# mLSTM cell and mixture of depths: exponents one step later, operands at the ends of steps, tables in the prologue, the tail in pieces

## The chip, the cores and the metric

One NeuronCore of a Trainium2 chip runs the kernel as one program. Its engines run side by side: TensorE (PE; its weight loads are listed as PEld), VectorE (DVE), ScalarE (ACT), GpSimd (POOL), and SyncE (SP), which issues most of the DMAs. Each engine takes its own instructions strictly in the order in which they were written; between engines, semaphores order them. The metric is the device time of one execution in microseconds (us).

## The reference, cut to what matters

Two blocks follow each other: a recurrent mLSTM cell over B=4, H=8, S=768, D=40, and a mixture-of-depths layer on its output x, seen as (4, 768, 320).

```python
# per batch and head, for t in 0..767
m_new  = max(f[t] + m, i[t]);  f_stab = exp(f[t] + m - m_new);  i_stab = exp(i[t] - m_new);  m = m_new
C = f_stab * C + i_stab * outer(v[t], k[t]);   n = f_stab * n + i_stab * k[t]
y[t] = sigmoid(o[t]) * (C @ q[t]) / max(abs(n @ q[t]), 1)
# then per batch, on x = y as (768, 320)
scores = x @ w_gate;   top = the 128 positions with the largest scores
out[top] = x[top] + sigmoid(scores[top]) * (relu(x[top] @ w1) @ w2);   out elsewhere = x
```

## The kernel before

The recurrence is computed by chunks of 128 positions, so there are 24 **steps** `(b, c)`: 4 batches of 6 chunks, numbered n = 0 to 23. All 8 heads of a chunk are handled together. A step is written by `step(n)`, and it works on three chunks at once: it ends chunk n, prepares the products of chunk n+1, and turns and weighs chunk n+2. No scheduler moves anything: the order in which the code is written is the order on each engine.

In a step, TensorE does in this order: `within` (L383, tile `pH`, 32 matmuls, the chunk's own attention), `exchange` for n+1 (L352 and L358, tile `pIC`: the carried state `C` against the queries, and the new part of the state from the scaled values `wv`), `products` (L326, `pS`, queries by keys), `weights` for n+2 (L304, `pW`, the exponents of the decay weights, from two operands `a_o` and `M_o`), in some steps `operands` (L234, `pO`, six small matmuls that place gate rows into those operands), then a piece of the mixture layer (`layer`: `pcol`, `pidx`, `pX`, `ph`, `py`, or `warm`, three matmuls into `pw` that nobody reads), the transposes of chunk n+2 (L284, `pt`) and `spread` (L412, `pb`, this chunk's scores as a row).

ScalarE takes the exponential of `pW` into `W` (L305), turns `pO` into `a_o` (L238) and `M_o` (L245, four instructions), copies `pt` into `T` (L285), applies the output gate to `so` (L295, L296), and copies `pb` into `sb` (L413). GpSimd zeroes the upper triangle of `W` (`causal`, L310), scales the values (`stated`, L317, `wv`), decays the state (`decay`, L340, `C`) and multiplies the gate by the reciprocal denominator (L398, `sor`). VectorE does the rest: `norm` (L390 to L396), `compare` (L419, `ge`, which scores are beaten), `result` (L403 `x`, L406 `sc`), `weighted` (L332, `P` = `pS` times `W`, which `pH` of the next step needs), and `exchanged` (L365 `num`, L375 `C`).

The operands of one chunk number c serve a pair of batches: `operands(0, c)` batches 0 and 1, `operands(1, c)` batches 2 and 3. The first kind is made in the prologue and in steps 1 to 3, the second in steps 4 to 9. They need tables `place`, of which the second pair is made on GpSimd after step 2 (L685 to L688). In steps 1 to 3 (`late`), the exponents of chunk n+2 are written at the end of the step, and `causal` and `stated` of that chunk behind them; in all other steps they stand in the middle.

PSUM holds 8 banks. `ps_t` has two buffers that `pt` and `pW` share, `ps_m` two that `pO`, `pb`, `pcol`, `pidx`, `pX`, `ph` and `py` share. A matmul into a shared buffer waits until its last reader is done.

After step 23 comes the tail (L712 to L740): the last comparison over all six chunks, ranks from counts and column sums (`pcol`), one-hot selections `sel`, the selected rows transposed by matmul (`pX`, L729), and the two layers of the last batch (`ph` L491, `py` L500).

Of the kernel before, what the change touches and what calls it, by code (L numbers as in the profile page):

```python
# [27 lines left out]
def kernel(  # L28
# [380 lines left out]
    def spread(u, sc, sb):  # L409

        pb = ps_m.tile([128, L], FP, name="pb", tag="m")
        nc.tensor.transpose(pb, sc[:, u:u + 1].to_broadcast([128, L]), ident)  # L412
        nc.scalar.copy(out=sb[:, u, :], in_=pb)  # L413

    def compare(u, sc, sb, ge, cnt):
# [5 lines left out]
                                       op0=OP.is_ge, op1=OP.mult, accum_out=cnt[:, u:u + 1])  # L421

    def columns_of(ge):

# [1 line left out]
        for t in reversed(range(NT)):
            for u in reversed(range(t, NT)):
                nc.tensor.matmul(pcol[:, t:t + 1], ge[:, GE[u] + t * L:GE[u] + (t + 1) * L], ones_b, start=(u == NT - 1),
                                 stop=(u == t))
# [253 lines left out]
    for n in range(2, N):  # L683
        step(n)
        if n == 2:  # L685
            for j in range(2):
                nc.gpsimd.memset(place[j][1], 0.0)
            places(1)  # L688
# [78 lines left out]
```

## Time and profile before

| | before |
|---|---|
| runs | 209.55, 209.54, 208.18 us, median 209.54 us |
| profiled execution, its own time | 209.95 us |
| its span, first to last instruction | 207.8 us |
| outside the span | 2.15 us |
| mean granted TensorE clock | 0.983 of full speed |
| PE busy | 180.4 us, 87% of the span |
| PEld busy | 148.2 us, 71% |
| DVE busy | 143.3 us, 69% |
| ACT busy | 102.8 us, 49% |
| POOL busy | 98.8 us, 48% |

A step can be read off the trace by the start of its `pH`. Steps 10 to 22 are nearly full on TensorE; the waits in front of TensorE stand in steps 1 to 9 and in the tail. In a row, the bracket at the end is the idle time of that engine just before the row, and what ended it.

### The profile page before, as it was taken

How to read it: one execution, taken by the hardware profiler on the slowest of the kernel's cores; microseconds unless marked ns; L12 is line 12 of the kernel's file. 1: busy time of each engine (PE TensorE's matmuls, PEld its weight loads, DVE VectorE, ACT ScalarE, POOL GpSimd, SP SyncE). 2: the span in 40 equal slices, each digit the busy share in tenths (PEclk: the TensorE clock that was granted, in tenths of full speed). 3: DMA queues.
4: the chain of work that ended last, by engine and by line, in shares of the span. 5: the costliest groups of instructions: out<-in, count | busy, mean ns of one | idle time of the engine just before them, and what ended most of it. 6: DMA issues, size and time to landing. Idle time of an engine off the chain costs nothing.

```text
span 207.8 us, 6508 instructions
## 1 busy us (share of the span) xinstructions
PE 180.4 (87%) x2597; PEld 148.2 (71%) x2606; DVE 143.3 (69%) x408; ACT 102.8 (49%) x246; POOL 98.8 (48%) x152
## 2 busy tenths in 40 slices
PE   6988877877698777979999999899999998988990
PEld 2467755656486756868887888788887897958870
DVE  7759964647885867765688869976886898664101
ACT  5682553935936864756555365546545543200210
POOL 6087406093646537533485466365657572022201
PEclk9999969999969999999999999999999999999999
DMA  4999999928999999994999689578992101010100
GB/s 82 122 172 141 143 182 169 153 29 196 155 180 166 214 145 238 160 155 51 159 139 148 104 148 166 106 126 119 145 152 65 36 32 35 32 35 33 32 0 32
DMA packets 105854, 24.37 MB, mean 117 GB/s; under 512 B 100640, under 2 KB 105248, under 8 KB 105824
## 3 DMA queue, kind: packets, MB, share of 16 engines
q1 hardware_dynamic: 105296, 22.60, 70.9%
q0 software_dynamic: 384, 1.31, 2.2%
q8 instruction: 20, 0.33, 0.8%
q14 instruction: 10, 0.08, 0.2%
q10 hardware_dynamic: 144, 0.05, 0.1%
HBM read 19.37 MB, written 4.59 MB: 115 GB/s over the span
## 4 chain that ended last, share of the span: by engine, by line
PE 33%; DVE 18%; issue 10%; POOL 7%; ACT 3%; DMA 3%; POOLq 1%; ACTq 0%
PE pH L383 8%; PE ph L491 5%; PE pS L326 5%; POOL sor L398 4%; PE pt L284 4%; PE py L500 3%; DVE P L332 3%; PE pIC L352 3%; ACT W L305 3%; DVE scr L406 2%; DVE num L390 2%; DVE x L403 2%; DVE den L394 2%; DVE ge L419 2%; DMA out_dram<-ye,idx 1%
## 5 line engine op out<-in xcount | busy, mean ns | idle before, releaser
L310 POOL TENSOR_SCALAR_AFFINE_SELECT W<-W 128x512 f32<-128x512 f32 x48 | 32.1, 693 | 34.0 <-ACT W L305 33.7
L305 ACT ACTIVATE W<-pW 128x512 f32<-128x512 f32 x48 | 26.1, 596 | 41.9 <-POOL sor L398 15.7
L398 POOL TENSOR_TENSOR sor<-so,rec 128x320 f32<-128x320 f32 x24 | 22.4, 934 | 41.4 <-DVE rec L396 40.0
L285 ACT COPY T<-pt 128x512 f32<-128x512 f32 x48 | 26.1, 595 | 18.1 <-PE pt L284 18.0
L332 DVE TENSOR_TENSOR P<-pS,W 128x512 f32<-128x512 f32 x48 | 30.7, 679 | 0.8 <-POOL W L310 0.8
L383 PEld LDWEIGHTS pH<-v,P 128*64 128x64 f32 x768 | 24.8, 138 | 7.3 <-DVE P L332 2.7
L383 PE MATMUL pH<-v,P 128*64 128x64 f32 x768 | 28.3, 226 | 1.7 <-DVE P L332 1.7
L326 PE MATMUL pS<-T 64*128 64x128 f32 x384 | 28.8, 291 | 0.0
L284 PE MATMUL pt<-ident,qk 128*128 128x128 f32 x192 | 26.0, 279 | 0.7 <-ACT W L305 0.7
L284 PEld LDWEIGHTS pt<-ident,qk 128*128 128x128 f32 x192 | 22.7, 144 | 5.1 <-ACT W L305 1.6
L326 PEld LDWEIGHTS pS<-T 64*128 64x128 f32 x384 | 24.1, 193 | 1.4
L491 PE MATMUL ph<-xeT,w 128*128 128x128 f32 x192 | 23.8, 280 | 1.5 <-ACT a_o L238 1.2
L491 PEld LDWEIGHTS ph<-xeT,w 128*128 128x128 f32 x192 | 22.1, 192 | 3.2 <-issue 1.4
L390 DVE TENSOR_TENSOR num<-num,pH 128x328 f32<-128x328 f32 x20 | 9.9, 495 | 17.6 <-PE pH L383 17.4
L403 DVE TENSOR_TENSOR x<-num,sor 128x320 f32<-128x320 f32 x20 | 11.1, 553 | 13.4 <-POOL sor L398 13.4
L419 DVE SCALAR_TENSOR_TENSOR ge<-sb,sc,earlier 128x128 bf16<-128x128 f32 (+5 forms) x24 | 18.4, 768 | 1.9 <-ACT sb L413 1.9
L500 PE MATMUL py<-w,hT 128*128 128x320 f32 x64 | 19.1, 439 | 0.0
L352 PE MATMUL pIC<-C,T 128*64 128x82 f32 x320 | 15.2, 236 | 1.9 <-DVE C L375 1.1
L358 PE MATMUL pIC<-wv,qk 128*64 128x41 f32 x320 | 12.8, 229 | 3.4 <-POOL wv L317 3.4
L317 POOL TENSOR_TENSOR wv<-v,cols 128x328 f32<-128x328 f32 x20 | 15.0, 751 | 0.0
L352 PEld LDWEIGHTS pIC<-C,T 128*64 128x64 f32 x320 | 12.7, 137 | 2.6 <-issue 1.5
L176 PE MATMUL pw<-earlier 128*128 128x512 bf16 x30 | 12.5, 478 | 2.2 <-POOL earlier L98 1.6
(121 smaller groups left out, 265.4 us busy)
## 6 DMA issues: line engine op xcount, KB each, us to landing
qk<-in_k_dram SPq DMA_DIRECT2D x24, 160.0 KB, 3.5
qk<-in_q_dram SPq DMA_DIRECT2D x24, 160.0 KB, 4.4
v<-in_v_dram SPq DMA_DIRECT2D x24, 160.0 KB, 4.9
so<-in_o_gate_dram SPq DMA_DIRECT2D x24, 160.0 KB, 4.6
out_dram<-x SPq DMA_DIRECT2D x24, 160.0 KB, 1.9
w<-in_moe_w_dram SPq DMA_DIRECT2D x2, 640.0 KB, 4.7
w<-in_moe_w_dram SPq DMA_DIRECT2D x2, 512.0 KB, 3.8
w<-in_moe_w_dram SPq DMA_DIRECT2D x1, 256.0 KB, 4.0
```

What stands on the lines that cost most here:

```text
L284: nc.tensor.transpose(pt[:, p, :], qk[:, j, 2 * p:2 * p + 2, :].rearrange("s a d -> s (a d)"), ident)
L285: nc.scalar.copy(out=T[:, j], in_=pt)
L305: nc.scalar.activation(out=W[:, h0:h0 + 4, :], in_=pW, func=AF.Exp)
L310: nc.gpsimd.affine_select(out=W[:, h0:h0 + 4, :], in_=W[:, h0:h0 + 4, :], compare_op=OP.is_ge, fill=0.0, base=0, pattern=[[0, 4], [1, L]], ...
L326: nc.tensor.matmul(pS[j][:, p, :], T[e, 0, p, :], T[e, 1, p, :], start=True, stop=True)
L332: nc.vector.tensor_tensor(out=P[:, :, j, :], in0=pS[j], op=OP.mult, in1=W.rearrange("p (n a) t -> p n a t", a=2)[:, :, j, :])
L352: nc.tensor.matmul(pI[t, 2 * p * D1:2 * (p + 1) * D1], T[:, 1, p, t], C[:, p].rearrange("e a d -> e (a d)"), start=True, stop=True)
L383: nc.tensor.matmul(pH[t, 2 * p + j, :], P[:, p, j, t], v1[:, 2 * p + j, :], start=True, stop=True)
L398: nc.gpsimd.tensor_tensor(out=sor, in0=so, in1=rec.unsqueeze(2).to_broadcast([128, H, D]), op=OP.mult)
L419: nc.vector.scalar_tensor_tensor(out=ge[:, GE[u]:GE[u + 1]], in0=sb.rearrange("p t l -> p (t l)")[:, 0:n], scalar=sc[:, u:u + 1], in1=earl ...
L491: nc.tensor.matmul(self.ph[:, f % 4, :], w1[:, j, f * 128:(f + 1) * 128], self.xeT[:, j, :], start=(j == 0), stop=(j == NDC - 1))
L500: nc.tensor.matmul(self.py, self.hT[:, f, :], w2[:, f, :], start=(f == 0), stop=(f == NFC - 1))
```

## The change

The change moves work and splits some of it; it leaves the arithmetic of the result as it was.

- **Exponents one step later.** `weights` of chunks 3, 4 and 5 stood at the end of steps 1, 2 and 3. Now they stand in steps 2, 3 and 4, right behind that step's `pH`, and their `causal` behind that step's `norm`. `stated` of these chunks (`wv`) no longer stands behind their `causal`.
- **Operands at the ends of six steps.** `operands(1, c)` moves from the middle of steps 4 to 9 to the end of steps 3 to 8, behind `spread`.
- **Tables in the prologue.** The second pair of `place` tables is zeroed on VectorE and filled on GpSimd in the prologue; two of three zeroings of `C` go.
- **Prologue.** Chunk 1's transposes come ahead of its exponents.
- **Tail in pieces.** The last `spread` and its copy go. The last comparison is split in two, the second read from PSUM; column sums over chunks 0 to 4 come early, those of chunk 5 go into a tile of their own (`pend`); the selection is made in six pieces instead of three; `pX` becomes three tiles, each copied as soon as it is there. Step 23 takes six of the eight `py` pieces instead of five.

```diff
@@ prologue
-    for j in range(2):
-        nc.vector.memset(place[j][0], 0.0)
+    for u in range(B // 2):
+        for j in range(2):
+            nc.vector.memset(place[j][u], 0.0)
...
     places(0)
-    for C in C_t:
-        nc.gpsimd.memset(C, 0.0)
+    nc.gpsimd.memset(C_t[1], 0.0)
+    places(1)
@@ step(n)
+        late = 0 < n < NT - 2
+        if 1 < n < NT - 1:
+            W[n + 1] = weights(*steps[n + 1])
         if n + 1 < N:
             give = exchange(*steps[n + 1], loaded[n + 1][0], T[n + 1], wv[n + 1])
...
-        if 4 <= n < 4 + NT:
-            operands(1, n - 4, beside=False)
         num, sor = norm(nums.get(n), pH, so)
+        if 1 < n < NT - 1:
+            causal(W[n + 1])
...
             if not late:
-                weighed(n + 2)
-        spread(c, *state[b][1][:2])
-        if late:
-            W[n + 2] = weights(*steps[n + 2])
+                causal(W[n + 2])
+            if n != 1:
+                stated(n + 2)
+        if n + 1 < N:
+            spread(c, *state[b][1][:2])
+        if 3 <= n < 3 + NT:
+            operands(1, n - 3, beside=False)
...
-        if late:
-            weighed(n + 2)
+        if n == 1:
+            stated(n + 2)
@@ tail
-    compare(u, sc, sb, ge, cnt)
-    own.second(5, NFC)
-    rank = ranks(columns_of(ge), cnt)
+    nc.vector.tensor_tensor(out=base[:, 0:u], in0=cnt[:, 0:u], in1=later[:, 0:u], op=OP.add)
+    sums_of(pcol, ge, u)
+    nc.vector.scalar_tensor_tensor(out=ge[:, GE[u]:GE[u] + n], ... accum_out=before)
+    nc.tensor.transpose(pb, sc[:, u:u + 1].to_broadcast([128, L]), ident)
+    own.second(6, NFC)
+    nc.vector.scalar_tensor_tensor(out=ge[:, GE[u] + n:GE[u + 1]], in0=pb, ... accum_out=cnt[:, u:u + 1])
+    for t in range(NT):
+        nc.tensor.matmul(pend[:, t:t + 1], ge[:, GE[u] + t * L:GE[u] + (t + 1) * L], ones_b, start=True, stop=True)
+    nc.vector.tensor_tensor(out=base[:, 0:u], in0=base[:, 0:u], in1=pcol, op=OP.subtract)
+    nc.vector.scalar_tensor_tensor(out=base[:, u:u + 1], in0=cnt[:, u:u + 1], scalar=before, in1=later[:, u:u + 1], ...)
+    nc.vector.tensor_tensor(out=rank, in0=base, in1=pend, op=OP.subtract)
...
-    for t in range(0, NT, 2):
-        select(sel, rank, t, t + 2)
+    for t in range(NT):
+        select(sel, rank, t, t + 1)
...
+        if j < 2:
+            copies[j](out=last.xeT[0:w, j], in_=pX[j][0:w])
     own.leave()
     select(sel_h, rank, 0, NT)
-    nc.scalar.copy(out=last.xeT[:, 0:NDC - 1], in_=pX[:, 0:NDC - 1])
-    nc.scalar.copy(out=last.xeT[0:w, NDC - 1], in_=pX[0:w, NDC - 1])
+    copies[2](out=last.xeT[0:w, 2], in_=pX[2][0:w])
```

On TensorE, around the end of step 2 and the start of step 3, there stood in the order before (`v_115` is chunk 3's value tile, `a_o_701` and `M_o_700` the operands of chunk 4):

```order
L284 MATMUL pt<-ident,qk_111 128x128 x8
L412 MATMUL pb<-ident,sc 128x128
L304 LDWEIGHTS a_o_701
L304 MATMUL pW<-M_o_700,a_o_701 128x512
L304 LDWEIGHTS a_o_701
L304 MATMUL pW<-M_o_700,a_o_701 128x512
L383 MATMUL pH<-v_115,P 64x64 x16
L352 MATMUL pIC<-C_118,T 64x82 x8
L358 MATMUL pIC<-wv,qk_111 64x41 x8
```

and there stands now:

```order
L286 MATMUL pt<-ident,qk_111 128x128 x8
L414 MATMUL pb<-ident,sc 128x128
L385 MATMUL pH<-v_115,P 64x64 x16
L306 LDWEIGHTS a_o_705
L306 MATMUL pW<-M_o_704,a_o_705 128x512
L306 LDWEIGHTS a_o_705
L306 MATMUL pW<-M_o_704,a_o_705 128x512
L354 MATMUL pIC<-C_118,T 64x82 x8
L360 MATMUL pIC<-wv,qk_111 64x41 x8
```

`pH` has moved ahead of the two `pW`; the same holds one step earlier, from step 1 into step 2.

On GpSimd, from `sor` of step 1 to `sor` of step 3, there stood before (`v_115` and `v_116` are chunks 3 and 4):

```order
L398 TENSOR_TENSOR sor<-so,rec 128x320
L310 AFFINE_SELECT W<-W 128x512 x2
L317 TENSOR_TENSOR wv<-v_115,cols_636 128x328
L340 TENSOR_TENSOR C_118<-C_117,cols_636 128x328
L398 TENSOR_TENSOR sor<-so,rec 128x320
L310 AFFINE_SELECT W<-W 128x512 x2
L317 TENSOR_TENSOR wv<-v_116,cols_636 128x328
L687 MEMSET placeM_131 96x384
L687 MEMSET placea_133 96x384
L143 TENSOR_SCALAR placeM_131<-head 96x4x4 x3
L143 TENSOR_SCALAR placea_133<-head 96x4x4 x3
L340 TENSOR_TENSOR C_119<-C_118,cols_636 128x328
```

and there stands now:

```order
L400 TENSOR_TENSOR sor<-so,rec 128x320
L319 TENSOR_TENSOR wv<-v_115,cols_635 128x328
L342 TENSOR_TENSOR C_118<-C_117,cols_635 128x328
L400 TENSOR_TENSOR sor<-so,rec 128x320
L312 AFFINE_SELECT W<-W 128x512 x2
L319 TENSOR_TENSOR wv<-v_116,cols_635 128x328
L342 TENSOR_TENSOR C_119<-C_118,cols_635 128x328
L400 TENSOR_TENSOR sor<-so,rec 128x320
L312 AFFINE_SELECT W<-W 128x512 x2
```

`wv`, `C` and `sor` no longer stand behind the `AFFINE_SELECT` of the same chunk, and the table work is gone from between.

On ScalarE, in the steps with operands (here steps 6 and 7), there stood before:

```order
L305 ACTIVATE W<-pW 128x512 x2
L238 ACTIVATE a_o_1188<-pO_1180,of 128x128
L245 ACTIVATE M_o_1187<-pO_1179,of_which,which 128x128 x4
L285 COPY T<-pt 128x512 x2
L295 ACTIVATE so<-so 128x320
L296 ACTIVATE so<-so 128x320
L413 COPY sb<-pb 128x128
```

and there stands now:

```order
L307 ACTIVATE W<-pW 128x512 x2
L287 COPY T<-pt 128x512 x2
L297 ACTIVATE so<-so 128x320
L298 ACTIVATE so<-so 128x320
L415 COPY sb<-pb 128x128
L240 ACTIVATE a_o_1266<-pO_1258,of 128x128
L247 ACTIVATE M_o_1265<-pO_1257,of_which,which 128x128 x4
```

The operands' five instructions moved from between `W` and `T` to behind `sb`. On TensorE their `pO` matmuls stand in the same steps between `pb` and the next step's `pH`; the second `pO` tile takes the PSUM buffer that `pb` holds until `sb` is copied.

## Rows read from the trace of the kernel before

**Rows 1.** Timeline, steps 1 to 3: start us, us, engine, line, operation, count, [idle before].
```profile
28.96 0.46 DVE L258 COPY cols<-pc 128x288 f32<-128x288 f32 x1
...
30.32 0.27 PE L412 MATMUL pb<-ident,sc 128*128 128x128 f32 x1
...
31.46 1.15 PE L383 MATMUL pH<-v,P 128*64 128x64 f32 x32
...
34.69 0.67 PE L358 MATMUL pIC<-wv,qk 128*64 128x41 f32 x16 [1.50 <-POOL wv L317]
...
36.22 0.49 DVE L403 TENSOR_TENSOR x<-num,sor 128x320 f32<-128x320 f32 x1 [1.30 <-POOL sor L398]
...
39.83 1.15 PE L383 MATMUL pH<-v,P 128*64 128x64 f32 x32
```
**Rows 2.** Timeline, step 4 into step 5: GpSimd beside VectorE, a wait of TensorE.
```profile
48.19 1.18 PE L383 MATMUL pH<-v,P 128*64 128x64 f32 x32
...
53.59 1.47 POOL L310 TENSOR_SCALAR_AFFINE_SELECT W<-W 128x512 f32<-128x512 f32 x2
53.66 0.90 DVE L403 TENSOR_TENSOR x<-num,sor 128x320 f32<-128x320 f32 x1 [0.61 <-POOL sor L398]
54.59 0.80 DVE L406 CUSTOM_DVE_ANT_0 scr<-x,wg 128x320 f32<-128x320 f32 x1
...
55.55 0.29 PE L412 MATMUL pb<-ident,sc 128*128 128x128 f32 x1 [1.73 <-DVE sc L406]
```
**Rows 3.** Timeline, end of step 7: TensorE and ScalarE around `pt` and `pb`.
```profile
74.20 0.33 PE L234 MATMUL pO<-M,placeM 32*128 32x128 bf16 x3
...
75.72 1.52 ACT L245 ACTIVATE M_o<-pO,of_which,which 128x128 bf16<-128x128 f32 x4
75.89 0.29 PE L448 MATMUL pidx<-token,sel 128*128 128x1 f16 x6 [1.36 <-ACT a_o L238]
...
76.68 1.04 PE L284 MATMUL pt<-ident,qk 128*128 128x128 f32 x8
...
77.76 1.15 PE L383 MATMUL pH<-v,P 128*64 128x64 f32 x32
...
79.17 0.25 ACT L413 COPY sb<-pb 128x128 f32<-128x128 f32 x1
```
**Rows 4.** Timeline, steps 9 and 11.
```profile
85.56 1.15 PE L383 MATMUL pH<-v,P 128*64 128x64 f32 x32
...
90.64 2.27 PE L491 MATMUL ph<-xeT,w 128*128 128x128 f32 x18 [1.16 <-ACT a_o L238]
...
93.82 1.15 PE L383 MATMUL pH<-v,P 128*64 128x64 f32 x32
...
100.08 1.15 PE L383 MATMUL pH<-v,P 128*64 128x64 f32 x32
...
105.78 1.28 PE L383 MATMUL pH<-v,P 128*64 128x64 f32 x32 [0.17 <-DVE P L332]
```
**Rows 5.** The page: granted TensorE clock in tenths, in 40 equal slices of the span.
```profile
PEclk9999969999969999999999999999999999999999
```
**Rows 6.** Timeline, the prologue: the first pair of tables on GpSimd.
```profile
2.44 0.69 POOL L143 TENSOR_SCALAR placeM<-head 96x16 bf16<-96x16 f32 x3 [0.38 <-DVE head L136]
```
**Rows 7.** Timeline, the tail.
```profile
184.75 0.08 DVE L406 DVE_READ_ACCUMULATOR2_ANT sc<- 128x1 f32 x1
...
187.62 1.10 DVE L441 TENSOR_TENSOR sel<-iota_f,rank 128x256 f32<-128x256 f32 x3
188.19 4.37 PE L729 MATMUL pX<-sel,x 128*128 128x128 f32 x36 [0.80 <-DVE sel L441]
...
193.14 1.13 PE L491 MATMUL ph<-xeT,w 128*128 128x128 f32 x8 [0.34 <-ACT xeT L734]
```
**Rows 8.** Groups by line and form: x count | busy us, mean ns of one.
```profile
L419 DVE SCALAR_TENSOR_TENSOR ge<-sb,sc,earlier 128x640 bf16<-128x640 f32 x4 | 3.3, 833 | 0.0
...
L419 DVE SCALAR_TENSOR_TENSOR ge<-sb,sc,earlier 128x128 bf16<-128x128 f32 x4 | 1.2, 310 | 0.0
```

More of the change, by code (lines that the diff above doesn't have):

```diff
@@ L321, in products @@
     def products(T):
-        pS = [ps_s.tile([128, NP, L], FP, name="pS") for _ in range(2)]
+        pS = [ps_s.tile([128, NP, L], FP, name="pS", tag="s") for _ in range(2)]
         for p in range(NP):
@@ L421, in compare, with sums_of @@
                                        op0=OP.is_ge, op1=OP.mult, accum_out=cnt[:, u:u + 1])
+    def sums_of(pcol, ge, n):
+        for t in reversed(range(n)):
+            for u in reversed(range(t, n)):
+                nc.tensor.matmul(pcol[:, t:t + 1], ge[:, GE[u] + t * L:GE[u] + (t + 1) * L], ones_b, start=(u == n - 1),
+                                 stop=(u == t))
     def columns_of(ge):
         pcol = ps_m.tile([128, NT], FP, name="pcol", tag="m")
[L426 to L429, printed above, removed]
+        sums_of(pcol, ge, NT)
         return pcol
@@ L551, in layer @@
         else:
-            layers[b - 1].second(0, 5)
+            layers[b - 1].second(0, 6)
     def weighed(n):
@@ L568, in step @@
             pS[n + 1] = products(T[n + 1])
-        late = 0 < n < NT - 2
         if 1 < n < NT - 2:
@@ L654 @@
     P[0] = weighted(pS[0], W[0])
+    turned(1)
     W[1] = weights(0, 1)
     weighed(1)
-    turned(1)
     give = exchange(0, 0, loaded[0][0], T[0], wv[0])
@@ L684 @@
         step(n)
[L685 to L688, printed above, removed]
         if n == 3:
@@ L714 @@
     own = layers[b - 1]
-    compare(u, sc, sb, ge, cnt)
-    own.second(5, NFC)
-    rank = ranks(columns_of(ge), cnt)
+    n = u * L
+    base = mod.tile([128, NT], FP, name="base", bufs=1)
+    nc.vector.tensor_tensor(out=base[:, 0:u], in0=cnt[:, 0:u], in1=later[:, 0:u], op=OP.add)
+    pcol = ps_t.tile([128, u], FP, name="pcol", tag="t")
+    sums_of(pcol, ge, u)
+    before = mod.tile([128, 1], FP, name="before", bufs=1)
+    nc.vector.scalar_tensor_tensor(out=ge[:, GE[u]:GE[u] + n], in0=sb.rearrange("p t l -> p (t l)")[:, 0:n],
+                                   scalar=sc[:, u:u + 1], in1=earlier[:, 0:n], op0=OP.is_ge, op1=OP.mult,
+                                   accum_out=before)
+    pb = ps_t.tile([128, L], FP, name="pb", tag="t")
+    nc.tensor.transpose(pb, sc[:, u:u + 1].to_broadcast([128, L]), ident)
+    own.second(6, NFC)
+    nc.vector.scalar_tensor_tensor(out=ge[:, GE[u] + n:GE[u + 1]], in0=pb, scalar=sc[:, u:u + 1], in1=earlier[:, n:],
+                                   op0=OP.is_ge, op1=OP.mult, accum_out=cnt[:, u:u + 1])
+    pend = ps_h.tile([128, NT], FP, name="pend", tag="h")
+    for t in range(NT):
+        nc.tensor.matmul(pend[:, t:t + 1], ge[:, GE[u] + t * L:GE[u] + (t + 1) * L], ones_b, start=True, stop=True)
+    nc.vector.tensor_tensor(out=base[:, 0:u], in0=base[:, 0:u], in1=pcol, op=OP.subtract)
+    nc.vector.scalar_tensor_tensor(out=base[:, u:u + 1], in0=cnt[:, u:u + 1], scalar=before, in1=later[:, u:u + 1],
+                                   op0=OP.add, op1=OP.add)
+    rank = mod.tile([128, NT], FP, name="rank")
+    nc.vector.tensor_tensor(out=rank, in0=base, in1=pend, op=OP.subtract)
     sel = work.tile([128, H, L], FP, name="sel", tag="W")[:, 0:NT, 0:K_]
@@ L723 @@
         nc.gpsimd.memset(last.xeT[w:, NDC - 1], 0.0)
-    pX = ps_m.tile([128, NDC, K_], FP, name="pX", tag="m")
-    for t in range(0, NT, 2):
-        select(sel, rank, t, t + 2)
+    for t in range(NT):
+        select(sel, rank, t, t + 1)
+    copies = (nc.scalar.copy, nc.scalar.copy, nc.vector.tensor_copy)
+    pX = [(ps_s, "s"), (ps_s, "s"), (ps_t, "t")]
+    pX = [pool.tile([128, K_], FP, name=f"pX{j}", tag=tag) for j, (pool, tag) in enumerate(pX)]
     for j, (d0, w) in enumerate(HW):
         for t in range(NT):
-            nc.tensor.matmul(pX[0:w, j, :], x_t[b, t][:, d0:d0 + w], sel[:, t], start=(t == 0), stop=(t == NT - 1))
+            nc.tensor.matmul(pX[j][0:w], x_t[b, t][:, d0:d0 + w], sel[:, t], start=(t == 0), stop=(t == NT - 1))
+        if j < 2:
+            copies[j](out=last.xeT[0:w, j], in_=pX[j][0:w])
     own.leave()
```

## The prediction

> **What bounds the kernel now.** I read the page first, for the share of each engine and the granted clock, then the list of waits, then the timeline step by step. TensorE is busy for 87% of the span, so the steps in the middle and at the end can hardly be shortened, and this change leaves steps 10 to 22 alone. What can go is idle time of TensorE, and it stands in three places. In steps 2 and 3 TensorE stands still for `wv` of the next chunk (1.50 us), and VectorE for `sor` (1.30 us), since both stand on GpSimd behind the `causal` of a late `W`; step 2 lasts from 31.46 to 39.83 [rows 1]. In steps 4 to 9 `pO` takes both buffers of `ps_m` in mid-step, so that what follows, `pidx` (1.36) or `ph` (1.16), waits until ScalarE has made the exponentials and `a_o` [rows 3, 4]; in step 4 `pb` waits 1.73 us for `sc` [rows 2]. And in the tail `pX` starts 3.4 us after the last `sc` [rows 7]. The granted clock falls twice, in the slices at 26 to 31 us and 57 to 62 us [rows 5]; the second fall stands just behind the 1.73 us wait [rows 2]. A mean granted clock of 0.983 over 207.8 us makes 3.5 us lost, 1.75 us a fall.
>
> **The change, part by part.** Times are on the axis of the profiled execution.
>
> *Prologue.* VectorE gets two more memsets, but what it makes first waits on TensorE's warming matmuls anyway. GpSimd makes the second tables right behind the first, six instructions, twice the 0.69 us of a row of three [rows 6], or 1.4 us, less two zeroings of `C`; this can hold VectorE up where both use memory. Bounds: 0 and 1.4. I take +0.2, near the lower end, since the tables come in small instructions and VectorE also waits for TensorE's answers there. That chunk 1's transposes come ahead of its exponents trades one buffer wait for another: 0.
>
> *Start of step 2.* `pH` no longer stands behind two `pW` that wait for `T`. Its `P` has long been there, so it starts when `pb` ends, 30.32 + 0.27 = 30.6 instead of 31.46 [rows 1]: **-0.85**.
>
> *Step 2.* `wv` now needs only `cols`, there at 28.96 + 0.46 = 29.4 [rows 1], on an idle GpSimd; the 1.50 us wait goes. Two paths lead to the next `pH`. On TensorE: `pH`, `pW`, two `pIC`, `pS`, `pO`, `warm`, `pt`, `pb` without a wait. From 85.56 to `ph` at 90.64, less its wait of 1.16, the first of these (with `pO`) take 3.9 us [rows 4]; `pidx` with `warm` took 0.8 (75.89 to 76.68) and `pt` with `pb` 1.1 (76.68 to 77.76) [rows 3]: 5.8, so 36.4. On VectorE: step 11, in which each step of VectorE's chain (`num`, `rec`, `sor`, `x`, `scr`, `P`) waits for the one before, lasted from 100.08 to 105.78, 5.7 us [rows 4]. Step 2 has a shorter comparison, but `causal` runs on GpSimd just beside `x` and `scr`; as these neighbours in step 4 they took 0.90 and 0.80 us [rows 2], against 0.49 for an `x` beside nothing [rows 1]. So 5.7 to 6.1, and I take 5.8 for both paths. The Trainium skill (GPSIMD Engine Reference, section 8, Key points) says that GpSimd shares its memory interfaces with VectorE where a VectorE instruction has two SBUF inputs, which speaks against placing `causal` there; rows 2 bear it out, and without it the VectorE path would be shorter than TensorE's by about half a microsecond and the sum would stay as it is. Step 2 takes 5.8 instead of 8.37: **-2.55**.
>
> *The new wait, steps 3 to 8.* The second `pO` tile now takes the buffer of `pb`, which is free only when ScalarE has copied it to `sb`, behind two `T` copies and two passes over `so`. On TensorE the next `pH` is queued behind it, and with it all of the step. From `pt` to the end of `sb` it is 79.17 + 0.25 - 76.68 = 2.74 us, from `pt` to `pH` it was 1.08 [rows 3]: 1.66 more, and the second half of `pO` behind it (0.33 [rows 3], of which I take 0.25, as its end overlaps `pH`), so **+1.9** in each of six steps. What hid `sb` was all of the next `pH` to `pS`; this cover is gone.
>
> *Step 3.* On the way to its `T` stands ScalarE: `pH` to `pO` 4.1, `a_o` and `M_o` 1.9, `T` to `sb` 2.1, `pO` 0.25: 8.35. Before, step 3 lasted 48.19 - 39.83 = 8.36 [rows 1, 2]: **0**. The waits for `wv` and `sor` go, the new one takes their place.
>
> *Steps 4 and 5.* Twice +1.9; gone are twice `pO` in mid-step (its two halves overlap; with 0.33 for one [rows 3] I take 0.4), the 1.73 us wait for `sc`, which now passes under `pt`, and the fall of the clock behind it, 1.75: **-0.5**.
>
> *Steps 6 to 8.* Each +1.9, less 0.4 and the wait behind `pO`, 1.36 in step 7 [rows 3] and alike in 6 and 8: **+0.45** in all.
>
> *Step 9.* No new wait any more, and no `pO`: 1.16 [rows 4] and 0.4 go: **-1.5**.
>
> *Tail.* From `sc` (184.83) to `pX` (188.19) it was 3.36 [rows 7]. Now: the first comparison over 640 columns 0.83, the second over 128 columns 0.31 [rows 8], each with 0.08 for its counter and a start; six short matmuls and their way back 0.4; one subtraction 0.2; one selection of 128 columns. No row shows this size: 256 columns take 0.37 [rows 7], so it lies between nothing and 0.37; I take 0.2. With the first addition (0.2) that is 2.4: -0.95. The `py` pieces and `pb` fit under the first comparison. From the end of `pX` (188.19 + 4.37 = 192.56) to `ph` (193.14) it was 0.58; two copies now run under `pX`, and the third beside `pidx`: 0.2, so -0.35. Together **-1.3**; between -1.5 and, if each of six selections takes 0.37 and holds up `pX`, -0.5.
>
> *Sum.* 0.2 - 0.85 - 2.55 + 0 - 0.5 + 0.45 - 1.5 - 1.3 = -6.05.
>
> *The clock.* Six new waits of 1.5 to 2 us, with only transposes and `pO` around them, are much like the one of 1.73 that was followed by a fall. But the waits of 1.50, 1.36 and 1.16 were not [rows 1, 3, 4, 5]. So a fall is about an even matter of where each lies. Likeliest are one or two in six; I take one, **+1.75**, between 0 and six (10.5). That leaves -4.3. From the profiled execution's own 209.95 that gives 205.65. This execution lies 0.4 above the median of the three runs, 209.54; against the median it would be 205.2. I say **205.5**.
>
> **The rivals.** (a) *The clock falls behind most of the new waits.* For it: their likeness to the wait in step 4, and that each waits a little longer than the ones that passed. Against it: three of the four waits shown passed. Four falls cost 7.0 and eat the whole sum: 210.9; six give 214.4. It decides from the fourth fall on; below that the kernel gains. This is the rival on the other side. (b) *The gain of step 2 shrinks*, since `causal` of the late `W` now stands behind `sor` and `P` waits for it. By the rows `causal` (1.47, from the end of `sor`) ends just before `scr` does, so it has no slack; if it took 0.7 longer in steps 2 and 3, and the prologue 1 us more, the time would be 208. (c) *No fall of the clock at all*: 203.9. For it: TensorE has little idle time elsewhere. (d) *The change does nothing in the steps*, the new wait taking all that steps 2 and 9 give: this needs +0.8 us in each of six steps, by `so` waiting for its DMA ahead of `sb`; then only the tail counts: 208.7 without a fall, 210.4 with one. Against it: ScalarE shows no wait for a DMA in front of `so` in the list of waits.
>
> **How the numbers follow.** The forecast with one or two falls (204.5 to 207.4) has 0.45, (c) with none (203 to 204.5) 0.22, (b) 0.12, (d) 0.08, (a) with three falls (about 209) 0.05, with four or more 0.08. The range that leaves no more than 2 in 10 out goes from 202.8 to 208.6: the lower end is (c) with the tail's best and no cost in the prologue, the upper one takes in (b) and ends at (d). One per cent, 2.1 us, is about what a measurement of this kernel can tell from no change. Faster than 207.4: the forecast, (c) and half of (b), with some of the rest, 0.76. Within one per cent: half of (b), (d) and three falls, 0.16. Slower than 211.6: five falls or more, 0.08.
>
> **What would show it.** Right: `pH` of step 2 starts at the end of `pb`; no wait of TensorE for `wv` in steps 2 and 3; step 2 lasts about 5.8 us and step 3 about 8.4; in steps 3 to 8 TensorE waits 1.4 to 2 us in front of the second `pO` for `sb`, and nothing waits behind `a_o` any more; step 9 lasts about 6.8; from the last `sc` to `pX` 2.4 us. Wrong: a granted clock of one half in more than two of the slices; `P` of steps 2 to 4 waiting for `causal`; steps 4 to 8 longer by more than 1 us each than before; six selections that hold up `pX`.

## The result and the profile after

The changed kernel took 203.37 us (median of four runs, 201.84 to 204.51), the kernel before 209.55 in the same sitting: a ratio of 0.971, 95% interval 0.964 to 0.979. A later sitting gave 204.16 against 209.76, ratio 0.972 (0.964 to 0.979); the ratios are of the means of the fast runs, which leaves one run of 205.39 and one of 211.81 out of the second. The forecast was 205.5, its range 202.8 to 208.6.

| | after | against before |
|---|---|---|
| profiled execution, its own time | 201.84 us | 8.1 us less |
| its span | 200.1 us | 7.7 us less |
| mean granted clock | 1.000 | 0.017 more |
| PE busy | 179.1 us, 89% of the span | 1.3 us less |
| DVE, ACT, POOL busy | 143.9, 103.7, 100.0 us | 0.6, 0.9, 1.2 us more |

The engines do as much work as before; 7.7 us of waiting and of half clock are gone. This profile happens to show the fastest of the four runs. Of the runs in which the granted clock lost equally much, those of the changed kernel are 5.0 us shorter: 203.4 against 208.4 us at a mean clock of 0.990 to 0.992, 204.6 against 209.7 at 0.982 to 0.984 (means over eight runs of the changed kernel and the 39 of the kernel before that stood beside the experiments). The rest of the 6.2 us is clock. The page's row of granted clocks after the change answers to [rows 5]: no slice of this execution is below 9.

```profile
PEclk9999999999999999999999999999999999999999
```

TensorE of the changed kernel at the start and end of step 2, from its timeline (columns as in [rows 1]), answers to [rows 1]:

```profile
29.62 0.27 PE L414 MATMUL pb<-ident,sc 128*128 128x128 f32 x1
29.82 1.15 PE L385 MATMUL pH<-v,P 128*64 128x64 f32 x32
...
31.84 0.61 PE L360 MATMUL pIC<-wv,qk 128*64 128x41 f32 x16
...
35.66 1.24 PE L385 MATMUL pH<-v,P 128*64 128x64 f32 x32
```

`pH` follows `pb` at once, the second `pIC` waits for no `wv`, and step 2 lasts 35.66 - 29.82 = 5.84 us. The new wait is there too. TensorE and ScalarE at the end of step 3:

```profile
41.51 0.28 PE L414 MATMUL pb<-ident,sc 128*128 128x128 f32 x1
41.73 0.33 PE L236 MATMUL pO<-a,placea 32*128 32x128 bf16 x3
43.72 0.32 PE L236 MATMUL pO<-M,placeM 32*128 32x128 bf16 x3 [1.66 <-ACT sb L415]
43.97 1.15 PE L385 MATMUL pH<-v,P 128*64 128x64 f32 x32
...
41.55 1.09 ACT L287 COPY T<-pt 128x512 f32<-128x512 f32 x2
42.49 0.52 ACT L297 ACTIVATE so<-so 128x320 f32<-128x320 f32 x1
43.04 0.47 ACT L298 ACTIVATE so<-so 128x320 f32<-128x320 f32 x1
43.42 0.25 ACT L415 COPY sb<-pb 128x128 f32<-128x128 f32 x1
```

The second `pO` starts when `sb` is copied, and `pH` behind it. Steps 4, 5, 7 and 8 show the same with 1.22, 0.90, 1.32 and 1.37 us; in step 6 the first `pO` waits instead, and for VectorE:

```profile
65.27 0.32 PE L236 MATMUL pO<-a,placea 32*128 32x128 bf16 x3 [1.18 <-DVE rank L442]
```

The tail, which answers to [rows 7]:

```profile
178.65 0.08 DVE L408 DVE_READ_ACCUMULATOR2_ANT sc<- 128x1 f32 x1
...
178.77 0.89 DVE L728 SCALAR_TENSOR_TENSOR ge<-sb,sc,earlier 128x640 bf16<-128x640 f32 x1
...
180.55 1.30 DVE L446 TENSOR_TENSOR sel<-iota_f,rank 128x128 f32<-128x128 f32 x6
180.90 4.40 PE L757 MATMUL pX<-sel,x 128*128 128x128 f32 x36 [0.58 <-DVE sel L446]
...
185.40 5.60 PE L496 MATMUL ph<-xeT,w 128*128 128x128 f32 x48
```

From the end of the last `sc` (178.65 + 0.08) to `pX` it is 2.17 us instead of 3.36, from the end of `pX` to `ph` 0.10 instead of 0.58, and a selection of 128 columns costs 1.30/6 = 0.22.

### The profile page after: what moved, and what is told of

Read it like the earlier page. It is cut to its first block, busy times and chain, and to the rows that moved or that the text cites. A ratio compares the mean times of both kernels' runs of the same rounds, so it can differ in the third digit from the quotient of the medians.

```text
span 200.1 us, 6525 instructions
## 1 busy us (share of the span) xinstructions
PE 179.1 (89%) x2606; PEld 146.1 (73%) x2606; DVE 143.9 (72%) x418; ACT 103.7 (52%) x245; POOL 100.0 (50%) x148
## 4 chain that ended last, share of the span: by engine, by line
PE 51%; DVE 19%; issue 9%; ACT 7%; DMA 5%; SPq 4%; POOL 3%; POOLq 1%
PE pH L385 11%; PE pS L328 8%; PE pt L286 6%; PE ph L496 5%; PE pIC L354 5%; PE py L505 3%; ACT T L287 3%; DVE P L334 3%; PE pw L178 3%; PE pIC L360 3%; POOL sor L400 3%; DVE scr L408 3%; PE pW L306 3%; DVE x L405 2%; SPq L93 2%
## 5 line engine op out<-in xcount | busy, mean ns | idle before, releaser
L400 POOL TENSOR_TENSOR sor<-so,rec 128x320 f32<-128x320 f32 x24 | 23.4, 977 | 46.4 <-DVE rec L398 44.9
L312 POOL TENSOR_SCALAR_AFFINE_SELECT W<-W 128x512 f32<-128x512 f32 x48 | 33.5, 723 | 16.2 <-ACT W L307 15.8
L328 PE MATMUL pS<-T 64*128 64x128 f32 x384 | 27.9, 285 | 0.0
L286 PEld LDWEIGHTS pt<-ident,qk 128*128 128x128 f32 x192 | 21.8, 141 | 5.4 <-issue 1.4
L328 PEld LDWEIGHTS pS<-T 64*128 64x128 f32 x384 | 23.3, 187 | 1.4
L405 DVE TENSOR_TENSOR x<-num,sor 128x320 f32<-128x320 f32 x20 | 11.9, 595 | 10.3 <-POOL sor L400 10.3
L421 DVE SCALAR_TENSOR_TENSOR ge<-sb,sc,earlier 128x128 bf16<-128x128 f32 (+5 forms) x23 | 16.5, 716 | 0.0
L408 DVE CUSTOM_DVE_ANT_0 scr<-x,wg 128x320 f32<-128x320 f32 x24 | 14.6, 609 | 0.8
L247 ACT ACTIVATE M_o<-pO,of_which,which 128x128 bf16<-128x128 f32 x36 | 13.6, 458 | 2.2 <-PE pO L236 1.4
L342 POOL TENSOR_TENSOR C<-C,cols 128x328 f32<-128x328 f32 x16 | 12.0, 749 | 4.5 <-PE pW L306 1.8
```

The source lines that it names most:

```text
L286: nc.tensor.transpose(pt[:, p, :], qk[:, j, 2 * p:2 * p + 2, :].rearrange("s a d -> s (a d)"), ident)
L312: nc.gpsimd.affine_select(out=W[:, h0:h0 + 4, :], in_=W[:, h0:h0 + 4, :], compare_op=OP.is_ge, fill=0.0, base=0, pattern=[[0, 4], [1, L]], ...
L400: nc.gpsimd.tensor_tensor(out=sor, in0=so, in1=rec.unsqueeze(2).to_broadcast([128, H, D]), op=OP.mult)
L408: nc.vector.tensor_tensor_reduce(out=scr, in0=x, in1=wg, scale=1.0, scalar=0.0, op0=OP.mult, op1=OP.add, accum_out=sc[:, c:c + 1])
```

## The experiments

Each kernel below was profiled, and the start of `pH` read off for every step. The table gives the us from one `pH` to the next (step 0 to 9), the start of the first `pH`, and the tail from the last `pH` to the end of the span. Steps 10 to 22 together took 86.27 to 86.32 in all of them. A fall, here and below, is a stretch in which the granted clock stands at one half. A star marks a number with a fall in it, of 3.4 us (6.8 us in step 5 of `exps_end`). In four profiles (`mid_step`, `one_tile`, `so_behind`, `rank_early`) the clock also falls in the last slice of the span, behind the last matmul of TensorE, where it costs nothing; it is not starred, but it lowers the mean clock a little (to 0.994 in `rank_early`, which has no other fall).

| kernel | pH 0 | 0 | 1 | 2 | 3 | 4 | 5 | 6 | 7 | 8 | 9 | tail |
|---|---|---|---|---|---|---|---|---|---|---|---|---|
| before | 14.88 | 6.35 | 10.23* | 8.37 | 8.36 | 7.92 | 6.43* | 8.28 | 6.94 | 7.80 | 8.26 | 27.75 |
| after | 15.49 | 6.57 | 7.76 | 5.84 | 8.31 | 7.44 | 6.84 | 7.73 | 7.42 | 7.59 | 6.70 | 26.11 |
| exps_end | 15.72 | 6.57 | 8.74 | 8.38 | 10.56* | 7.23 | 9.53* | 7.74 | 7.42 | 7.93 | 6.70 | 26.10 |
| exps_only | 14.59 | 6.36 | 7.75 | 5.83 | 6.61 | 6.73 | 5.83 | 9.06* | 6.94 | 7.82 | 8.25 | 27.74 |
| mid_step | 16.17* | 7.18* | 7.76 | 5.84 | 6.39 | 6.74 | 5.83 | 8.48* | 7.62* | 7.82 | 8.25 | 26.10 |
| one_tile | 16.09* | 7.17* | 7.76 | 5.83 | 6.49 | 6.68 | 5.83 | 7.84 | 5.94 | 6.41 | 6.70 | 26.10 |
| so_behind | 15.64 | 6.58 | 9.28* | 5.83 | 7.36 | 6.58 | 6.03 | 7.60 | 6.57 | 6.72 | 6.70 | 26.11 |
| prologue_order | 14.99 | 6.36 | 9.35* | 5.83 | 8.22 | 7.44 | 6.83 | 7.74 | 7.42 | 7.58 | 6.70 | 26.10 |
| step6_ahead | 14.74 | 6.35 | 7.75 | 5.84 | 6.49 | 6.68 | 5.81 | 7.67 | 5.95 | 6.41 | 6.70 | 26.10 |
| rank_early | 14.79 | 6.35 | 7.76 | 5.83 | 6.50 | 6.68 | 5.81 | 6.45 | 6.38 | 7.01 | 6.70 | 26.11 |
| after_again | 15.53 | 7.12* | 8.77* | 6.39* | 8.23 | 8.91* | 6.85 | 7.73 | 7.42 | 7.58 | 6.70 | 26.15 |

**The exponents, undone alone (exps_end).**

```diff
-        if 1 < n < NT - 1:
-            W[n + 1] = weights(*steps[n + 1])
...
-        if 1 < n < NT - 1:
-            causal(W[n + 1])
...
+        if late:
+            W[n + 2] = weights(*steps[n + 2])
...
+        if late:
+            weighed(n + 2)
```

> The changed kernel with the exponents of chunks 3, 4 and 5 back at the ends of steps 1, 2 and 3, their wv behind their causal, all else as changed: this edit alone undone. Theory (wv and sor behind causal on GpSimd make the long steps): step 1 about 0.85 longer at full clock, step 2 about 2.5 longer, step 3 longer by up to 1.5; 3.4 to 5 us in all, 205.5 to 207 at full clock, and the waits pIC for wv (1.5) and x for sor (1.3) are back. Rival (the gain of steps 1 and 2 came from the tables in the prologue and from a fall of the clock that happened to be absent): under 1.5 us longer at full clock. If the fall of the clock at 26 to 31 us is bound to the late exponents it is back here, 1.5 us more.

209.88 us against 209.86 for before: ratio 1.000 (0.996 to 1.005). Taking this one edit back takes back the whole gain, but part of that is clock: at a mean clock of 0.991 it ran 207.6 us and at 0.983 208.7 (one run each), against 203.4 and 204.6 of the changed kernel, so the edit itself is worth 4.0 to 4.2 us, as the theory had it. Step 1 is 0.98 longer, step 2 2.54, both without a fall of the clock, and step 3 has its waits again. TensorE in steps 2 and 3 and at the end of step 3:

```profile
34.26 0.67 PE L360 MATMUL pIC<-wv,qk 128*64 128x41 f32 x16 [1.51 <-POOL wv L319]
...
42.64 0.67 PE L360 MATMUL pIC<-wv,qk 128*64 128x41 f32 x16 [1.51 <-POOL wv L319]
...
49.72 0.32 PE L236 MATMUL pO<-M,placeM 32*128 32x128 bf16 x3 [0.65 <-ACT sb L415]
```

The theory stands. The fall in step 1 did not come back in this profile, so it is not bound to the late exponents; but with them TensorE's clock fell more often than in the changed kernel: its ten runs had mean clocks of 0.962 to 0.991, those of the changed kernel 0.974 to 1.000.

**The exponents alone, on the kernel before (exps_only).**

```diff
+        if 1 < n < NT - 1:
+            W[n + 1] = weights(*steps[n + 1])
...
+        if 1 < n < NT - 1:
+            causal(W[n + 1])
...
-                weighed(n + 2)
+                causal(W[n + 2])
+            if n != 1:
+                stated(n + 2)
...
-        if late:
-            W[n + 2] = weights(*steps[n + 2])
...
```

> The kernel before with nothing but the exponents of chunks 3, 4 and 5 one step later (wv ahead of causal); operands in mid-step, tables after step 2, old prologue, old tail. Theory (this edit alone carries the gain in the steps, as the run with the operands back in mid-step suggests): step 1 about 1.0 shorter at full clock, step 2 about 2.5, step 3 about 1.9 to 2.0 (no new wait takes its place there), steps 4 and 5 about 1.2 (the wait of pb for sc of 1.73 goes), steps 6 to 9 and the tail as before: 6.5 less, about 203. Rival (without the tables in the prologue, their eight instructions on GpSimd after step 2 take the gain of step 3 back): step 3 near 8, about 204.5 to 205.

203.14 us against 209.76, ratio 0.971 (0.965 to 0.977): the same as the whole change, and at equal mean clock 1.1 to 1.3 us less than it (202.1 against 203.4, 203.6 against 204.6). Step 3 falls to 6.61, steps 4 and 5 to 6.73 and 5.83, although the tables are still made on GpSimd after step 2; that rival falls. What is left to wait for around step 4, at its start and at its end, is VectorE (step 5 shows the same with 0.26 and 0.18):

```profile
41.14 1.24 PE L383 MATMUL pH<-v,P 128*64 128x64 f32 x32 [0.26 <-DVE P L332]
47.31 0.29 PE L412 MATMUL pb<-ident,sc 128*128 128x128 f32 x1 [0.48 <-DVE sc L406]
```

The wait for `sc` that was 1.73 [rows 2] is 0.48 here.

**The operands back in mid-step (mid_step).**

```diff
+        if 4 <= n < 4 + NT:
+            operands(1, n - 4, beside=False)
...
-        if 3 <= n < 3 + NT:
-            operands(1, n - 3, beside=False)
```

> The changed kernel with operands(1, c) back in the middle of steps 4 to 9, all else as changed: this edit alone undone. Theory (the new wait at the ends costs about what the two buffers in mid-step cost before): step 3 about 1 us shorter than in the changed kernel, steps 4 to 8 within 1.5 us of it, step 9 back at 8.2 (1.5 longer); in all the time of the changed kernel within 1 us. Rival (the move of the operands carries the gain of steps 4 to 9): 3 us longer or more.

201.59 us, ratio 0.962 (0.955 to 0.970), 1.8 faster than the changed kernel, though the two intervals overlap: this edit of the change costs time. Step 3 is 1.92 shorter, steps 4 and 5 together 1.71; step 9 is 1.55 longer, with the wait of [rows 4] back (`ph` for `a_o`, 1.16). Steps 6 to 8 hold a fall of the clock here; before, with the same order, they took 23.02, after 22.74. That makes 1.92 + 1.71 - 0.28 - 1.55 = 1.8 for the move. That the medians differ by just as much is in part luck, as these runs lost more clock (means of 0.971 to 0.988) than those of the changed kernel (0.974 to 1.000). The theory's "within 1 us" was too narrow, and the rival had the wrong sign.

**Both `pO` in one buffer (one_tile).**

```diff
-        pO = [ps_m.tile([128, L], FP, name=f"pO{j}", tag="m") for j in range(2)]
+        if u == 0:
+            pO = [ps_m.tile([128, L], FP, name=f"pO{j}", tag="m") for j in range(2)]
+        else:
+            both = ps_m.tile([128, 2, L], FP, name="pO", tag="m")
+            pO = [both[:, j] for j in range(2)]
```

> The changed kernel, with both pO tiles of steps 3 to 8 side by side in one buffer of ps_m, so that only one buffer is taken beside pb and the second half does not wait for sb. The trace of the changed kernel shows TensorE waiting in front of the second pO 1.66, 1.22, 0.90, 1.32 and 1.37 us (steps 3, 4, 5, 7, 8) and 1.18 us in step 6 for rank. Theory (the new wait is on the path, and nothing else stands close behind it): steps 4, 5, 7, 8 shorten by nearly the wait, step 3 by at most 0.8 since VectorE is busy there for 7.44 of 8.31 us, step 6 not at all; 4.5 us less in all, 197 at full clock. Rival (P on VectorE or W on ScalarE is late next): under 2 us less, and the list of waits shows pH waiting for P in these steps instead.

196.64 us, ratio 0.939 (0.932 to 0.947); 195.9 in the two runs at full clock, 5.9 less than the changed kernel at full clock. Steps 3, 4, 5, 7 and 8 shorten by 1.82, 0.76, 1.01, 1.48 and 1.18, together 6.25, about the waits for `sb` that the trace had shown (6.47). Step 6 keeps its wait for `rank`:

```profile
63.27 0.32 PE L240 MATMUL pO<-a,placea 32*128 32x128 bf16 x3 [1.33 <-DVE rank L446]
63.43 0.33 PE L240 MATMUL pO<-M,placeM 32*128 32x128 bf16 x3
```

The theory stands and was too careful about step 3: it now takes 6.49, with VectorE busy for 5.70 us, so the 7.44 busy us that VectorE had there in the changed kernel were no bound of the step. The Trainium skill (PSUM — Partial Sum Buffer, "PSUM bank collisions raise a hardware error") warns of an engine that reads a bank while TensorE writes it. In this trace `a_o` never starts before the last `pO` matmul of its tile has ended (0.03 us behind it in step 6, over 0.6 in the others), so this run shows no such collision.

**ScalarE's order instead (so_behind).**

```diff
             turned(n + 2)
-            gated(n + 2)
+            if not 3 <= n < 3 + NT:
+                gated(n + 2)
...
         if 3 <= n < 3 + NT:
+            gated(n + 2)
             operands(1, n - 3, beside=False)
```

> The changed kernel with ScalarE's two passes over so behind the copy sb instead of ahead of it in steps 3 to 8; the two pO tiles stay apart. Theory (the second pO waits for sb, and sb stands behind T and so on ScalarE): the wait shrinks by about 0.9 to 1.0, from 1.66, 1.22, 0.90, 1.32, 1.37 to 0.7, 0.3, 0, 0.4, 0.4, and step 6, which waits for rank on VectorE, stays at 7.7; 4 us less in all at full clock. Rival (ScalarE is full there, and what is moved behind sb delays a_o, M_o and W of the next step by as much): the waits shrink, but the steps do not, under 1 us less.

One run, 199.0 us, with a fall in step 1. The waits for `sb` are 0.80, 0.37, none, 0.47 and 0.52, each 0.85 to 0.90 less:

```profile
44.44 0.32 PE L236 MATMUL pO<-M,placeM 32*128 32x128 bf16 x3 [0.80 <-ACT sb L415]
51.02 0.32 PE L236 MATMUL pO<-M,placeM 32*128 32x128 bf16 x3 [0.37 <-ACT sb L415]
```

Steps 3 to 8 are 4.5 shorter in all, and none of them is longer. So the new wait is made of ScalarE's queue, as the prediction had it: two `T`, two `so`, then `sb`. The share of the two `so` is shown by this run; that of the two `T` is read from the trace alone.

**Chunk 1's order in the prologue (prologue_order).**

```diff
-    turned(1)
     W[1] = weights(0, 1)
     weighed(1)
+    turned(1)
```

> The changed kernel with chunk 1's exponents ahead of its transposes again, as before; the tables stay in the prologue. In the changed kernel the first pH starts at 15.49, before at 14.88, though pS of chunk 0 came 0.25 earlier (10.36 for 10.61). Theory (the order costs, the tables do not: pt waits for the DMA of q, then pW for T): pH starts at 14.6 to 14.7, and the whole kernel is 0.7 to 0.9 us faster. Rival (the tables or the memsets cost it): pH stays near 15.4 and the time does not move. Second rival: pH is earlier but step 1 or 2 gives it back while waiting for a DMA.

202.39 us, ratio 0.968 (0.962 to 0.974); at a mean clock of 0.990 to 0.992, 202.3 against 203.4 of the changed kernel. The first `pH` comes 0.50 earlier, step 0 is 0.21 shorter, and the second `pH` stands at 21.35 against 22.06 after and 21.23 before. So the order costs 0.7, and what is left for the tables and the rest of the prologue is 0.1. In the changed kernel TensorE waits for the DMA of `q`, and the exponents stand behind:

```profile
12.86 0.63 PE L286 MATMUL pt<-ident,qk 128*128 128x128 f32 x4 [0.56 <-DMA qk<-in_q_dram]
13.42 0.38 PE L306 MATMUL pW<-M_o,a_o 32*128 32x512 bf16 x1
14.16 0.37 PE L306 MATMUL pW<-M_o,a_o 32*128 32x512 bf16 x1 [0.36 <-ACT T L287]
```

**The changed kernel once more, for the clock (after_again).** No edit.

> The changed kernel itself, unchanged, for the falls of the granted clock. In its four runs so far the mean clock was 1.000, 0.992, 0.991 and 0.983 and the span 200.1, 201.6, 201.7 and 202.8. Theory (the falls are a matter of chance from run to run at places where TensorE has waited before): again none to two falls in a run, a fall in the profile at another place than 26 or 57 us or none at all, 1.3 to 1.6 us more for each. Rival (a fall belongs to a place in the program): the same slices in every profile.

Seven of its runs, of both sittings, fall into groups: a mean clock of 1.000 with 201.84 and 201.90, of 0.991 or 0.992 with 203.31 to 203.56, of 0.982 or 0.983 with 204.51 and 204.77. That is none, one or two falls, 1.6 us for the first and 1.2 for the second by the groups' means. The profiled execution of this label, 205.39 at 0.974, has three, in steps 0, 1 to 2 and 4:

```profile
PEclk9996987996999999999999999999999999999999
```

The third one lies just behind a new wait, by the timeline of TensorE:

```profile
45.79 0.32 PE L236 MATMUL pO<-M,placeM 32*128 32x128 bf16 x3 [1.66 <-ACT sb L415]
```

Three stretches of TensorE around it (stretch and its us, PE busy, granted clock, DMA share, GB/s):

```profile
45.00:46.00 1.00, 0.21 (x3) 1.00 0.98 346
46.00:49.50 3.50, 3.50 (x53) 0.55 1.47 161
49.50:51.00 1.50, 1.50 (x20) 0.91 0.48 49
```

In the first profile the same wait of 1.66 was followed by no fall. So the places are not fixed, as the theory says, but falls do not come just anywhere either. In the steps every fall of the eleven profiles began behind a wait of TensorE of over 1 us: in step 1 behind the wait for `M` of 1.27 to 1.36 (before, prologue_order, so_behind, after_again), in steps 3 and 4 behind one of 1.5 to 1.7 (exps_end, after_again), in steps 5 and 6 behind one of 1.15 to 1.73 (before, exps_end, exps_only, mid_step). TensorE of the kernel before in step 1, where its first fall begins at 26.69:

```profile
26.49 0.58 PE L234 MATMUL pO<-M,placeM 32*128 32x128 bf16 x2 [1.27 <-DVE M L220]
```

The fall began 0.1 to 2.0 us behind the end of the wait. In all, the eleven profiles have 51 waits of TensorE of over 1 us in steps 1 to 9, and 10 of them were followed by a fall. All but one of the waits named were passed without a fall in other profiles; the exception is the wait of `pb` for `sc` in step 4, which was followed by a fall both times that it lasted over 1 us (1.73 in before, 1.28 in exps_end). What decides between a fall and none is not shown. The three falls at 14.7 to 15.6 us come where chunk 1's transposes stand first in the prologue.

**A version meant to beat both (step6_ahead).** `one_tile` with the order of `prologue_order`, and in step 6 the operands ahead of the column sums:

```diff
+        if n == NT:
+            operands(1, 3, beside=False)
         if b > 0 and c == 0:
             pcol = columns_of(state[b - 1][1][2])
...
-        if 3 <= n < 3 + NT:
+        if 3 <= n < 3 + NT and n != NT:
             operands(1, n - 3, beside=False)
```

> A version meant to beat both: the changed kernel with both pO tiles in one buffer, chunk 1's exponents ahead of its transposes in the prologue, and in step 6 the operands ahead of the column sums pcol, so that pO does not wait there for rank (1.33 us in the run with one buffer). Theory: 6.1 less from one buffer, 0.8 from the prologue, 0.9 from step 6 (7.84 to about 6.9): at full clock 192.5, with one or two falls of the clock 194 to 195. Rival for step 6 (a_o and M_o ahead of T on ScalarE make T, sb and so the next step late): step 6 or 7 gives it back, 0.9 more.

194.39 us, ratio 0.930 (0.925 to 0.935). Five of six runs were at full clock. The third part failed: step 6 took 7.67, since the wait only moved to `pb`:

```profile
61.08 0.32 PE L418 MATMUL pb<-ident,sc 128*128 128x128 f32 x1 [1.31 <-DVE rank L446]
```

**`rank` ahead of `P` in step 6 (rank_early).**

```diff
+        if n == NT:
+            rank = ranks(pcol, state[b - 1][1][3])
         if n + 1 < N:
             P[n + 1] = weighted(pS[n + 1], W[n + 1])
```

> As the version before it (one buffer for both pO tiles, chunk 1's exponents ahead of its transposes), but with step 6's operands behind spread again and the two small rank instructions of step 6 on VectorE ahead of P instead of behind C. In the run with the operands ahead of pcol the wait for rank went to pb (1.31 us), since pb took the buffer of pcol, and step 6 kept 7.67. Theory (it is pcol's buffer that is waited for, and rank is late since it stands behind P, num and C): rank is done about 2.2 us earlier, the wait of 1.3 goes, P is 0.35 later and still in time, step 6 takes 6.3 to 6.7, and the time is 1.0 to 1.3 below that run: 193.2 where no fall of the clock comes. Rival (P or ScalarE is late next): step 6 stays above 7.2 or step 7 takes it.

194.48 us, ratio 0.929 (0.924 to 0.934): no better. Step 6 fell to 6.45 as expected, but steps 7 and 8 took 0.43 and 0.60 more. GpSimd's gather in step 7, which takes over 1.2 us of GpSimd with `causal` and `wv` behind it, began at nearly the same time in both versions, since VectorE came no earlier to what stands in front of it. VectorE and GpSimd of this kernel:

```profile
60.74 0.65 DVE L381 TENSOR_TENSOR C<-C,pIC 40x164 f32<-40x164 f32 x2
61.42 0.96 DVE L450 TENSOR_TENSOR sel<-iota_f,rank 128x768 f16<-128x768 f32 x1
62.41 0.49 DVE L396 TENSOR_TENSOR num<-num,pH 128x328 f32<-128x328 f32 x1
63.63 0.72 POOL L404 TENSOR_TENSOR sor<-so,rec 128x320 f32<-128x320 f32 x1 [0.65 <-DVE rec L402]
...
65.33 0.15 DVE L462 TENSOR_SCALAR idx<-pidx 128x1 uint32<-128x1 f32 x1
65.78 1.23 POOL L464 DMA_INDIRECT xe<-out_dram,idx  x1 [1.43 <-DMA w<-in_moe_w_dram]
```

and of `step6_ahead`:

```profile
62.53 0.49 DVE L396 TENSOR_TENSOR num<-num,pH 128x328 f32<-128x328 f32 x1 [0.27 <-PE pH L389]
63.75 0.72 POOL L404 TENSOR_TENSOR sor<-so,rec 128x320 f32<-128x320 f32 x1 [2.31 <-DVE rec L402]
...
65.45 0.15 DVE L462 TENSOR_SCALAR idx<-pidx 128x1 uint32<-128x1 f32 x1
65.90 1.23 POOL L464 DMA_INDIRECT xe<-out_dram,idx  x1 [1.43 <-DMA w<-in_moe_w_dram]
```

The bracket of the gather names a DMA, but it names only what ended last by the profile, and that is another load from profile to profile, or `idx` itself (in `after`). What stays is the distance to `idx`, the row numbers that the gather needs: in step 7 of all eleven profiles the gather starts 0.3 us behind the end of `idx`, here 65.48 and 65.78, in `step6_ahead` 65.60 and 65.90. `idx` stands on VectorE behind `sc`, which needs `x` and so `sor`, and `sor` waits for `rec`. In this kernel `pH` of step 7 had ended at 61.32, but VectorE came to it only at 62.41, behind the exchange and `sel`; in `step6_ahead` VectorE still waited for `pH` and came to it at 62.53. So of the 1.2 us that TensorE gained in step 6, VectorE passed on 0.12. Step 7 is longer since its first `pIC`, which reads `C`, starts at 61.53, just behind VectorE's `C` (60.74 + 0.65 = 61.39); in `step6_ahead` `C` was there before `pH`. TensorE of step 8 then waits 0.42 for `wv`, which stands behind the gather. So the rival's second half holds: the later steps take it, and what they stand on is VectorE. A run with less work on VectorE there was not made.

## Why the prediction was right or wrong, point by point

The time lies inside the range, and the mechanisms named for steps 2, 3 and 9, the new wait and the tail are those that the runs show. Luck had a part in it: the prologue cost 0.6 more than forecast and steps 6 to 8 gave 0.7 more, and in steps 4 and 5 two errors cancel. The profiled executions, 207.85 and 200.11 us of span, differ by 7.7; the forecast's sum was 6.05 before the clock was added. Without the fall in step 1, the measured terms make 6.28.

| term | forecast | measured | |
|---|---|---|---|
| prologue and step 0 | +0.2 | +0.83 | 0.61 + 0.22 |
| start of step 2, at full clock | -0.85 | -0.98 | step 1, exps_end against after |
| the fall of the clock in step 1 | 0 | -1.49 | 10.23 - 8.74 |
| step 2 | -2.55 | -2.53 | |
| step 3 | 0 | -0.05 | |
| steps 4 and 5 | -0.5 | -0.07 | 14.35 to 14.28 |
| steps 6 to 8 | +0.45 | -0.28 | 23.02 to 22.74 |
| step 9 | -1.5 | -1.56 | |
| tail | -1.3 | -1.64 | |

- **Prologue.** The tables were right (0.1). "Trades one buffer wait for another: 0" for chunk 1's order was wrong: 0.7. It left out that the transposes need chunk 1's `q`, whose DMA was still under way (the wait of 0.56 above), and that everything behind them then waits too.
- **Steps 2, 3 and 9** came out within 0.1, by the mechanisms named: `wv` and `sor` no longer behind `causal`, the new wait in the place of the old ones in step 3, no `pO` in step 9.
- **The new wait.** Forecast 1.9 a step; from `pt` to the next `pH` it is now 3.34, 3.10, 3.10, 3.03, 3.09 and 3.04 in steps 3 to 8, against 1.08 [rows 3], so 2.0 to 2.3. In step 6 it is not `sb` but `rank` that is waited for; the prediction did not see that `pO` there takes the buffer of `pcol`.
- **Steps 4 and 5** came out within 0.43 by luck, through two errors that cancel. The credit was 1.73 + 1.75 = 3.48 for the wait for `sc` and the fall behind it; exps_only shows 14.35 - 12.56 = 1.79, since 0.48 of the wait stays and the fall cost only 6.43 - 5.83 = 0.60 in a step where TensorE alone did not set the pace (without the fall it waits there for VectorE). The price was 2 x (1.9 - 0.4) = 3.0; mid_step shows 1.71, since without the new wait these steps wait for VectorE instead (0.48 for `sc`, 0.26 for `P`, the same as in exps_only).
- **Steps 6 to 8** were 0.7 better. In step 6 TensorE of the kernel before also waited for `T` in front of `pIC`, and that wait, which the forecast had not counted, is gone too; that it makes the whole 0.7 is not shown. TensorE of the kernel before:

```profile
64.45 0.79 PE L352 MATMUL pIC<-C,T 128*64 128x82 f32 x16 [0.76 <-ACT T L285]
```

- **Tail.** The mechanism held, and each part was a little better: 2.17 us from `sc` to `pX` for 2.4, and 0.10 in front of `ph` for 0.2, with 0.22 for a selection taken as 0.2; 1.19 + 0.48 makes the 1.6.
- **The clock** is the step that failed. The sum took away the fall in steps 4 and 5, kept the one in step 1, and added one for the new waits: two falls in all. Two falls is what the kernel before has in its median run (39 runs beside the experiments, mean clocks 0.969 to 0.992, median 0.982), while the changed kernel has about one. The price was off too: 1.75 a fall was forecast, and the runs show 1.6 for the first and 1.2 for the second. Taken fall for fall the forecast reads 205.65 with two, 203.9 with one, 202.15 with none; measured were 204.5 to 204.8, 203.3 to 203.6 and 201.8 to 201.9. So of the 2.1 us between forecast and median, 1.2 is one fall too many; the rest is its price and the errors of the other terms.
- **The rivals.** (a) six falls behind six new waits: in the two profiles of the changed kernel there was one fall behind twelve such waits, and in that of prologue_order none behind six more. (b) `causal` too late: `P` of step 2 started at 34.88, where `scr` ended, and step 2 took 5.84. (c), no new fall, was worked out at 203.9 and is in effect what happened. (d) `so` waiting for its DMA: not seen; so_behind showed that the two passes themselves make 0.85 to 0.90 of each wait. The case against (a) counted four waits of the kernel before, three of them passed; it left out that the first fall, too, stood behind a wait (1.27 us for `M` in step 1). And the chance of 0.08 for slower than 211.6 was that of four falls or more, though four make only 210.9.
- **What the forecast did not say at all** is how the parts stand to each other. The exponents alone give the whole gain (203.14); the tail adds 1.6, and the new place of the operands (1.8) and of chunk 1's transposes (0.7) take back that and 0.9 more, which agrees with the 1.1 to 1.3 us between the two at equal mean clock.

## What to carry to other kernels

When two tiles take both buffers of a rotating pool, look at who holds the next one: putting both halves into one tile gave 5.9 us here, almost as much as the whole change, and it needed no further buffer. Price each edit of a change by itself, as the sum of a good part and a bad one looks like a modest good one. Before you believe a wait that the profile puts down to a DMA, look whether the waiting instruction keeps a fixed distance to something else that it needs. And count the falls of the clock on both sides of a comparison. The versions with one or two waits of over 1 us in front of TensorE mostly had fewer falls, but not by a rule: mid_step had five such waits and the changed kernel six, and yet it lost more clock (means of 0.971 to 0.988 against 0.974 to 1.000). A fall cost 1.5 to 1.6 us in step 1 and 0.6 in step 5, where TensorE also waits for VectorE.
